# The second expert's output product as seven block products of 512 columns

## The chip, the cores and the metric

The kernel runs on one core of a Trainium2 chip. The metric is device time of one execution in microseconds. TensorE is PE in the rows, its weight loads PEld; VectorE is DVE, ScalarE is ACT, GpSimd is POOL, and SyncE (SP) issues all transfers between the chip's memory and the core's on-chip buffers.

## The reference

Attention over 4 x 576 = 2304 tokens gives 512 features per token. Two experts follow, each of the form below, the first one behind a normalisation. The change touches the second.

```python
def _moe2_ref(x, w_gate, w_val, w_out) -> np.ndarray:
    g = x @ w_gate
    silu = g * (1.0 / (1.0 + np.exp(-g)))
    val = x @ w_val
    return (silu * val @ w_out).astype(np.float32)
```

x is 2304 x 512, the hidden layer has 1536 features, and the result is 2304 x 512.

## The kernel before

Everything is kept transposed: features on the 128 partitions, tokens along the columns. The tokens form five groups (TGROUPS): four of 512 and one of 256. The 1536 hidden features are twelve chunks f of 128 (KF). Products are made in three parts: each float32 operand is split into a rounded high part H (a copy on ACT) and the remainder L (a subtraction on DVE or POOL, L1120), and a product is H.H + H.L + L.H, three matmuls that accumulate in one PSUM bank.

The first layer of the second expert runs over f (`pair_unit` and `plain_unit`). For each f the four wide groups form two pairs, and gate and value of a pair are computed together as a 2 x 2 block product with seven products instead of eight, each of six wide matmuls (L1274). Copies of banks go to buffers on ACT (`keep`, L1280), additions of banks run on DVE (`add`, L1284), one sum of two buffers at L1310. `gated` then makes silu(g) times v as Tanh on ACT (L1289) and two DVE operations (L1291, L1294); the factor one half that this leaves out is applied at the very end (L1141, L1143). The hidden block, 128 x 512, is stored to memory (`h2_d`, L1296). The 256-token group takes 24 narrow matmuls (L1325) and the operations of `hidden`. Weights of f + 2 are fetched, converted from 8-byte floats (L1070 on ACT, L1074 on DVE), summed (L1191) and split (L1198, L1201) by `load_w2`.

The output stage multiplies the hidden layer by w_out (`out_layer`, `out_mm`). For each group it reads twelve hidden blocks back (L1160), splits each (L1117, L1120), and issues twelve matmuls per block: four row blocks of the result by three parts (L1132). Four banks accumulate over the twelve blocks, and are copied out and stored (`out_store`). w_out is loaded and split (`load_o`, L1051, L1053) while the first layer ends and the output stage begins.

The order on each engine is fixed when the program is built: every operation is recorded with its engine, an estimated duration, its operands and a priority, and `Plan.run` lists them greedily, lowest priority number first among those that are ready by its estimates. Each engine then works through its own list in order, and an operation that must wait holds up what stands behind it on that engine.

## Time and profile before

| | |
|---|---|
| runs | 1100.15, 1098.49, 1096.84 us (median 1098.49) |
| the profiled execution | 1097.84 us, of which the span of its records is 1096.1 |
| PE busy | 1078.8 us of the span, 6580 matmuls |
| DVE, ACT, POOL busy | 675.9, 583.5, 208.1 us |
| transfers | 131.42 MB, mean 120 GB/s, none above 512 KB |
| second expert, first layer | 664.1 to 947.4 us of the span |
| second expert, output stage | 940.7 to 1092.6 us, its first rows between the last of the first layer |

The span is what the records cover; the run's own time is 1.7 us longer. Busy time is the union of an engine's records. Matmuls are pipelined, so a single one's record is longer than the distance from one to the next.

### The profile page before, as it was taken

How to read it: one execution, taken by the hardware profiler on the slowest of the kernel's cores; microseconds unless marked ns; L12 is line 12 of the kernel's file. 1: busy time of each engine (PE TensorE's matmuls, PEld its weight loads, DVE VectorE, ACT ScalarE, POOL GpSimd, SP SyncE). 2: the span in 40 equal slices, each digit the busy share in tenths (PEclk: the TensorE clock that was granted, in tenths of full speed). 3: DMA queues.
4: the chain of work that ended last, by engine and by line, in shares of the span. 5: the costliest groups of instructions: out<-in, count | busy, mean ns of one | idle time of the engine just before them, and what ended most of it. 6: DMA issues, size and time to landing. Idle time of an engine off the chain costs nothing.

```text
span 1096.1 us, 19019 instructions
## 1 busy us (share of the span) xinstructions
PE 1078.8 (98%) x6580; PEld 973.5 (89%) x6580; DVE 675.9 (62%) x1755; ACT 583.5 (53%) x1266; POOL 208.1 (19%) x300
## 2 busy tenths in 40 slices
PE   7899999999999999999999999999999999999998
PEld 5599999999999999999978889888888888888888
DVE  7798788796787766652344437676677566632222
ACT  5877777766775764531244336544554455543222
POOL 4344444423333220210000000121122111000000
PEclk9999999999999999999999999999999999999999
DMA  5974444333332213641233333232232223654342
GB/s 159 301 257 136 112 122 126 117 114 94 98 108 75 80 41 121 182 137 47 70 121 96 99 97 93 91 113 85 101 139 101 88 92 129 210 180 132 99 135 96
DMA packets 81616, 131.42 MB, mean 120 GB/s; under 512 B 12848, under 2 KB 42544, under 8 KB 81520
## 3 DMA queue, kind: packets, MB, share of 16 engines
q1 hardware_dynamic: 81520, 130.20, 37.9%
q8 instruction: 52, 0.85, 0.3%
q14 instruction: 44, 0.36, 0.1%
HBM read 97.05 MB, written 33.10 MB: 119 GB/s over the span
## 4 chain that ended last, share of the span: by engine, by line
PE 84%; DMA 3%; DVE 2%; ACT 1%; issue 1%; POOLq 0%; POOL 0%; ACTq 0%; DVEq 0%; SPq 0%
PE mo L921 23%; PE mo L1132 12%; PE mo L1274 10%; PE sps L1274 8%; PE tp L1132 6%; PE sps L1132 6%; PE tp L708 4%; PE tp L692 4%; PE sps L628 4%; PE mo L1325 3%; DMA cvs<-in_w_o 2%; PE tp L1274 1%; PE mo L828 1%; ACT cvy L1070 1%; DVE cvs L1074 0%
## 5 line engine op out<-in xcount | busy, mean ns | idle before, releaser
L921 PE MATMUL mo<-xH,H 128*128 128x320 f32 (+1 forms) x768 | 228.0, 297 | 0.8 <-DVE x L905 0.8
L921 PE MATMUL mo<-xL,H 128*128 128x320 f32 (+1 forms) x768 | 227.8, 297 | 0.0
L921 PE MATMUL mo<-xH,L 128*128 128x320 f32 (+1 forms) x768 | 227.7, 297 | 0.0
L921 PEld LDWEIGHTS mo<-xH,H 128*128 128x128 f32 x768 | 144.1, 188 | 1.9 <-DVE x L905 1.0
L921 PEld LDWEIGHTS mo<-xL,H 128*128 128x128 f32 x768 | 144.3, 188 | 0.7 <-issue 0.2
L921 PEld LDWEIGHTS mo<-xH,L 128*128 128x128 f32 x768 | 144.3, 188 | 0.4
L665 ACT ACTIVATE sc<-sc,col 128x512 f32<-128x512 f32 (+4 forms) x160 | 96.0, 601 | 64.3 <-DVE col L654 63.7
L1120 DVE TENSOR_TENSOR hL<-hh,hH 128x512 fp32r<-128x512 f32 (+1 forms) x90 | 58.2, 651 | 114.8 <-ACT hH L1117 114.6
L1117 ACT ACTIVATE hH<-hh 128x512 fp32r<-128x512 f32 (+1 forms) x90 | 52.5, 587 | 114.9 <-PE mo L1132 55.9
L928 ACT ACTIVATE t<-mo 128x256 f32<-128x256 f32 (+1 forms) x108 | 43.1, 399 | 58.5 <-PE mo L921 57.9
L930 DVE SCALAR_TENSOR_TENSOR t<-t,mo 128x256 f32<-128x256 f32 (+1 forms) x108 | 48.1, 445 | 40.4 <-ACT t L928 39.4
L692 PE MATMUL tp<-ident,sc 128*128 128x128 f32 x432 | 65.5, 276 | 0.0
L700 DVE TENSOR_TENSOR pTB<-tp,pTB 128x512 fp32r<-128x512 f32 (+1 forms) x96 | 54.4, 575 | 14.5 <-ACT pTB L697 12.4
L933 DVE TENSOR_TENSOR hh<-t,mo 128x256 f32<-128x256 f32 (+1 forms) x108 | 48.0, 445 | 18.9 <-PE mo L921 18.0
L1280 ACT ACTIVATE u<-sps 128x512 f32<-128x512 f32 x48 | 28.7, 598 | 54.1 <-PE sps L1274 54.0
L1132 PE MATMUL mo<-hL,oH 128*128 128x512 f32 (+1 forms) x144 | 54.4, 378 | 0.0
L628 PE MATMUL sps<-kHH,qst 128*128 128x288 f32 (+4 forms) x160 | 54.2, 346 | 0.0
L1132 PE MATMUL mo<-hH,oH 128*128 128x512 f32 (+1 forms) x144 | 54.0, 377 | 0.0
L1132 PE MATMUL mo<-hH,oL 128*128 128x512 f32 (+1 forms) x144 | 53.8, 377 | 0.0
L1289 ACT ACTIVATE u<-u 128x512 f32<-128x512 f32 x48 | 29.7, 633 | 43.7 <-DVE u L1284 43.7
L654 DVE CUSTOM_DVE_ANT_0 sc<-sps,cb 128x384 f32<-128x384 f32 (+3 forms) x112 | 48.9, 443 | 6.4 <-PE sps L628 5.3
L697 ACT ACTIVATE pTB<-tp 128x512 fp32r<-128x512 f32 (+1 forms) x96 | 47.0, 502 | 10.9 <-PE tp L692 5.9
(221 smaller groups left out, 2795.3 us busy)
## 6 DMA issues: line engine op xcount, KB each, us to landing
hh<-h_d SPq DMA_DIRECT2D x72, 256.0 KB, 2.6
cvs<-in_w_gv SPq DMA_DIRECT2D x28, 511.8 KB, 4.6
h_d<-u SPq DMA_DIRECT2D x48, 256.0 KB, 2.0
cvs<-in_w_o SPq DMA_DIRECT2D x24, 511.8 KB, 4.0
h_d<-hh SPq DMA_DIRECT2D x84, 128.0 KB, 1.9
raw<-in_w_gv SPq DMA_DIRECT2D x20, 511.8 KB, 5.7
lq<-in_qk SPq DMA_DIRECT2D x32, 288.0 KB, 3.6
cb<-cum_d SPq DMA_DIRECT2D x32, 288.0 KB, 3.5
```

Of the source, the lines that this page charges most:

```text
L628: op(PE, c_mm(n), lambda en, pt=pt, o=o, c=c, n=n, z=z, kk=kk: en.matmul(pt()[:, :n], qst[j]()[:, o:o + 128], kk()[:, c:c + n], start=z == ...
L654: op(DVE, c_tt(w), lambda en: en.tensor_tensor_reduce(out=sc()[:m, c:c + w], in0=pt()[:m, c - at:c - at + w], in1=bias()[:m, c + off:c + o ...
L665: op(ACT, c_act(o + m, 2) + 35, lambda en: en.activation(sc()[:m, :o + m], sc()[:m, :o + m], ACTF.Exp, scale=-1.0, bias=col()[:m, 0, t:t + 1],
L692: op(PE, C_TR, lambda en, pt=pt, a=a, m=m, kb=kb, t=t: en.transpose(pt()[:, a:a + P], self.sc[t]()[:, kb * P:kb * P + P], ident()), r=[sel ...
L700: op(DVE, c_tt(n), lambda en, pt=pt, a=a, d0=d0, n=n, kn=kn: en.tensor_tensor(out=L()[:kn, d0:d0 + n], in0=pt()[:kn, a:a + n], in1=f32(H() ...
L921: op(PE, c_mm(n), lambda en, a=a, x=x, c=c, k=k, i=i: en.matmul(ps()[:, :n], a()[:, c], x()[:, k, :n], start=(k == 0 and i == 0), stop=(k ...
L930: op(DVE, c_tt(n), lambda en: en.scalar_tensor_tensor(out=t()[:, :n], in0=t()[:, :n], scalar=1.0, in1=gp()[:, :n], op0=ALU.add, op1=ALU.mu ...
L933: op(DVE, c_tt(n), lambda en: en.tensor_tensor(out=hh()[:, :n], in0=t()[:, :n], in1=vp_()[:, :n], op=ALU.mult), r=[vp_, t], w=[hh], pri=pri)
L1117: op(ACT, c_act(n) + 35, lambda en: en.activation(H(), src(), ACTF.Copy), r=[src], w=[H], pri=pri)
L1120: lambda en: en.tensor_tensor(out=L(), in0=src(), in1=f32(H()), op=ALU.subtract),
L1132: op(PE, c_mm(n), lambda en, d=d, c=c, w=w, x=x, i=i: en.matmul(acc_[d]()[:, :n], Wo[w]()[:, c], HL[x](), start=(f == 0 and i == 0), stop= ...
L1274: op(PE, c_mm(n), lambda en, w=w, xx=xx, cut=cut, kk=kk, i=i: en.matmul(ps()[:, :n], W[w]()[:, cut], xx(), start=first and kk == 0 and i == 0,
```

## The change

The output product is made for each pair of groups as a 2 x 2 block product too: w_out in four blocks (768 hidden features by 256 outputs), the hidden layer of the pair in four blocks (768 features by 512 tokens). Seven products of six chunks replace eight, with sums S1 to S4 of the w_out blocks and differences T1 to T4 of the hidden blocks. For f from 0 to 5 `pair_unit` stores B12, B11 and their difference T1; for f from 6 to 11 it reads B12 and T1 of f - 6 back and stores B22, B21, T3, T2 and T4. All go to memory as rows of 128 x 512 (`row_d`). The blocks and sums of w_out are made during f = 0 to 5 (`store_o`), stored to `wo_d`, and read back and split later (`fetch_o`) into places that the first layer leaves free. `strassen_out` reads the rows in the order of the products (`fetch_row`, a rotation of four buffers each for the row and its two parts), each row feeding six matmuls, two output row blocks by three parts. The 256-token group is multiplied plainly, last, as before. `gated` and `plain_unit` use Silu on ACT and one DVE product; the factor one half falls away. A buffer that the program reserves for software-made transfer descriptors is cut to 1024 bytes, which makes room.

```diff
-    def pair_unit(f, W, X, groups, pri):
+    def pair_unit(f, W, X, p, pri):
...
-        def gated(g, t, ps, v, gi):
-            op(ACT, c_act(n), lambda en: en.activation(t(), g(), ACTF.Tanh, scale=0.5),
-               r=[g], w=[t], pri=-1.0e4)
-            op(DVE, c_tt(n), lambda en: en.scalar_tensor_tensor(
-                out=t(), in0=t(), scalar=1.0, in1=g(), op0=ALU.add, op1=ALU.mult),
-               r=[g, t], w=[t], pri=-1.0e4, port=True)
-            op(DVE, c_tt(n), lambda en: en.tensor_tensor(out=t(), in0=t(), in1=v(), op=ALU.mult),
-               r=[t, ps], w=[t], pri=-1.0e4, port=ps is u3)
-            op(SP, 4 * P * n, lambda en: en.dma_start(out=h2_d[gi][f], in_=t()), r=[t],
-               w=[(f"h2_d{gi}", f)], pri=-1.0e4)
+        def gated(g, ps, v):
+            op(ACT, c_act(n), lambda en: en.activation(g(), g(), ACTF.Silu),
+               r=[g], w=[g], pri=-1.0e4)
+            op(DVE, c_tt(n), lambda en: en.tensor_tensor(out=g(), in0=g(), in1=v(), op=ALU.mult),
+               r=[g, ps], w=[g], pri=-1.0e4, port=ps is u3)
+
+        def store(name, src):
+            op(SP, 4 * P * n, lambda en: en.dma_start(out=row_d[p, name][k6], in_=src()), r=[src],
+               w=[(f"row{p}{name}", k6)], pri=-1.0e4)
+
+        def fetch(name, dst):
+            op(SP, 4 * P * n, lambda en: en.dma_start(out=dst(), in_=row_d[p, name][k6]),
+               r=[(f"row{p}{name}", k6)], w=[dst], pri=pri)
+
+        def less(out, a, b):
+            op([(POOL, c_ptt(n)), (DVE, c_tt(n) + 60)], 0, lambda en: en.tensor_tensor(
+                out=out(), in0=a(), in1=b(), op=ALU.subtract), r=[a, b], w=[out], pri=-1.0e4,
+               port=True)
+        if f >= K6:
+            fetch("T1", t1)
+            fetch("B12", t2)
...
-        gated(u2, t2, u3, u3, groups[1])
+        gated(u2, u3, u3)
         product(b, "A22", "T4", False)
-        gated(p1, t1, b, lambda: b()[:, :n], groups[0])
+        gated(p1, b, lambda: b()[:, :n])
+        if f < K6:
+            store("B12", u2)
+            store("B11", p1)
+            less(p5, u2, p1)
+            store("T1", p5)
+        else:
+            store("B22", u2)
+            store("B21", p1)
+            less(t2, u2, t2)
+            store("T3", t2)
+            less(t1, u2, t1)
+            store("T2", t1)
+            less(p5, p1, t1)
+            store("T4", p5)
...
+        hh = m2buf(f"tmp{f % 2}", [P, 512], F32, "hh")
+        op(ACT, c_act(n), lambda en: en.activation(hh()[:, :n], gp()[:, :n], ACTF.Silu),
+           r=[gp], w=[hh], pri=-1.0e4)
+        op(DVE, c_tt(n), lambda en: en.tensor_tensor(
+            out=hh()[:, :n], in0=hh()[:, :n], in1=vq()[:, :n], op=ALU.mult),
+           r=[hh, vq], w=[hh], pri=-1.0e4)
+        op(SP, 4 * P * n, lambda en: en.dma_start(out=rest_d[f], in_=hh()[:, :n]),
+           r=[hh], w=[("rest_d", f)], pri=-1.0e4)
...
+    K6 = KF // 2
+    ROWS = ("B11", "B12", "B21", "B22", "T1", "T2", "T3", "T4")
+    row_d = {(p, name): dram.tile([K6, P, 512], F32, name=f"row{p}{name}")
+             for p in range(NPAIR) for name in ROWS}
+    rest_d = dram.tile([KF, P, 256], F32, name="rest_d")
+    O_BLOCKS = ("A11", "A21", "A12", "A22", "S1", "S2", "S3", "S4")
+    wo_d = dram.tile([2, 4, P, K6, 256], F32, name="wo_d")
+
+    def store_o(i, pri):
+
+        vals, osum = (buf("ex", f"ex{z}", [P, 1024], F32, ("vals", "osum")[z]) for z in range(2))
+        for z in range(2):
+            load_raw(w2_o[(i + K6 * z) * P:(i + K6 * z + 1) * P, :], raws[z], pri,
+                     lambda z=z: vals()[:, 512 * z:512 * z + 512], (vals, z))
+        a11, a21, a12, a22 = (Part(vals, k // 2, lambda t, k=k: t[:, 256 * k:256 * k + 256])
+                              for k in range(4))
+        s1, s2, s3, s4 = (Part(osum, k, lambda t, k=k: t[:, 256 * k:256 * k + 256])
+                          for k in range(4))
+        for out, a, b, sign in ((s1, a21, a22, ALU.add), (s2, s1, a11, ALU.subtract),
+                                (s3, a11, a21, ALU.subtract), (s4, a12, s2, ALU.subtract)):
+            op([(POOL, c_ptt(256)), (DVE, c_tt(256) + 60)], 0,
+               lambda en, out=out, a=a, b=b, sign=sign: en.tensor_tensor(
+                   out=out(), in0=a(), in1=b(), op=sign), r=[a, b], w=[out], pri=pri, port=True)
+        for z, t in ((0, vals), (1, osum)):
+            op(SP, 4 * P * 1024, lambda en, z=z, t=t: en.dma_start(
+                out=wo_d[z].rearrange("q p k c -> p q k c")[:, :, i],
+                in_=t().rearrange("p (q c) -> p q c", c=256)), r=[t], w=[("wo_d", (i, z))],
...
-        pair_unit(f, W2[f], X2[0], (0, 1), P3 + 40 * f)
+        pair_unit(f, W2[f], X2[0], 0, P3 + 40 * f)
         plain_unit(f, W2[f], rest, 2 * NPAIR, 256, P3 + 40 * f + 10)
-        pair_unit(f, W2[f], X2[1], (2, 3), P3 + 40 * f + 20)
-
-    W2o = []
-    w2o_wide = {}
+        if f < K6:
+            store_o(f, P3 + 40 * f + 19)
+        pair_unit(f, W2[f], X2[1], 1, P3 + 40 * f + 20)
...
+    plan.live["ex"] = []
+    seats = [seat("ex", f"ex{i}", [P, 1024], 1)[0] for i in range(3)]
+    for tag in w2_tags[0]:
+        seats += seat("m2", tag, [P, 2048], 2)
+    free_w = [f"{z}{f}" for f in range(KF) for z in "HL"]
+    for tag in free_w[:14]:
+        seats += seat("w", tag, [P, 1024], 1)
+    last_seats = [seat("w", tag, [P, 1024], 1)[0] for tag in free_w[14:17]]
...
+    def fetch_o(name, seats, pri, stages=stages):
+
+        q = O_BLOCKS.index(name)
+        for j, (H, L) in enumerate(seats):
+            st = stages[nstage[0] % len(stages)]
+            nstage[0] += 1
+            op(SP, 4 * P * 512, lambda en, st=st, j=j: en.dma_start(
+                out=st().rearrange("p (k c) -> p k c", c=256),
+                in_=wo_d[q // 4, q % 4][:, 2 * j:2 * j + 2]),
+               r=[("wo_d", (i, q // 4)) for i in (2 * j, 2 * j + 1)], w=[st], pri=pri)
+            split(st, 512, H, L, pri)
+        return seats
...
+    PRODUCTS = (("A11", "B11"), ("S1", "T1"), ("S2", "T2"), ("S4", "B22"), ("S3", "T3"),
+                ("A12", "B21"), ("A22", "T4"))
...
+    deep = {"h": [("o", "hh0"), ("o", "hh1"), ("m2", "tmp0"), ("m2", "tmp1")],
+            "H": [("o", "hH0"), ("o", "hH1"), ("o", "oH4"), ("o", "oH5")],
+            "L": [("o", "hL0"), ("o", "hL1"), ("o", "oL4"), ("o", "oL5")]}
...
+    def fetch_row(src, key, n, pri):
+
+        hh, H, L = (dring(z, F32 if z == "h" else F32R) for z in "hHL")
+        def view(b):
+            return Part(b, None, lambda t: t[:, :n])
+        hh, H, L = view(hh), view(H), view(L)
+        op(SP, 4 * P * n, lambda en: en.dma_start(out=hh(), in_=src), r=[key], w=[hh], pri=pri)
+        split(hh, n, H, L, -1.0e4, any_engine=False)
+        return H, L
...
+        def product(ps, first, claims=()):
+            a, x = PRODUCTS[step[0]]
+            at = pri + step[0]
+            step[0] += 1
+            for kk in range(K6):
+                H, L = fetch_row(row_d[p, x][kk], (f"row{p}{x}", kk), n, at)
+                for m in range(2):
+                    for i, (z, xx) in enumerate(((0, H), (0, L), (1, H))):
+                        part, w = weight(a, kk, m, z)
+                        op(PE, c_mm(n), lambda en, m=m, w=w, xx=xx, kk=kk, i=i: en.matmul(
+                            ps[m]()[:, :n], w(), xx(), start=first and kk == 0 and i == 0,
+                            stop=kk == K6 - 1 and i == 2, skip_group_check=not first),
+                           r=[part, xx], w=[ps[m]] if kk or m or i else [*ps, *claims], pri=at)
...
+        product(b, True, c if p == 0 else [])
+        keep(p1, b)
+        product(c, True)
+        keep(p5, c)
+        product(b, False)
+        keep(u2, b)
+        product(c, False)
+        add(u2, c)
+        store(u2, 0, 2 * p + 1)
+        product(b, False)
+        keep(u3, b)
+        for m in range(2):
+            op([(POOL, c_ptt(n)), (DVE, c_tt(n))], 0, lambda en, m=m: en.tensor_tensor(
+                out=u3[m](), in0=u3[m](), in1=p5[m](), op=ALU.add), r=[u3[m], p5[m]], w=[u3[m]],
+               pri=-1.0e4, port=True)
+        store(u3, 1, 2 * p + 1)
+        product(d, True)
+        add(p1, d)
+        store(p1, 0, 2 * p)
...
-    for gi, (t0, n) in enumerate(TGROUPS):
-        a = out_layer(gi, h2_d, f"h2_d{gi}", W2o, P4 + 100 * gi, gi % 2 == 0, True)
...
```

Where the orders differ. PE in the output stage; `oH`, `hH` are high parts of a row (their `L` the remainders), `mo` are banks. Before, one row feeds twelve matmuls:

```order
L1132 MATMUL mo3_11499<-hH0_11528,oH_10835 128x512
L1132 MATMUL mo3_11499<-hL0_11533,oH_10835 128x512
L1132 MATMUL mo3_11499<-hH0_11528,oL_10842 128x512
L1132 MATMUL mo0_11506<-hH0_11528,oH_10835 128x512
L1132 MATMUL mo0_11506<-hL0_11533,oH_10835 128x512
L1132 MATMUL mo0_11506<-hH0_11528,oL_10842 128x512
L1132 MATMUL mo2_11515<-hH0_11528,oH_10835 128x512
L1132 MATMUL mo2_11515<-hL0_11533,oH_10835 128x512
L1132 MATMUL mo2_11515<-hH0_11528,oL_10842 128x512
L1132 MATMUL mo1_11521<-hH0_11528,oH_10835 128x512
L1132 MATMUL mo1_11521<-hL0_11533,oH_10835 128x512
L1132 MATMUL mo1_11521<-hH0_11528,oL_10842 128x512
```

After, six, and the next row follows:

```order
L1531 MATMUL mo2_11272<-oH4_11401,wo_11050 128x512
L1531 MATMUL mo2_11272<-oL4_11406,wo_11050 128x512
L1531 MATMUL mo2_11272<-oH4_11401,wo_11050 128x512
L1531 MATMUL mo1_11281<-oH4_11401,wo_11050 128x512
L1531 MATMUL mo1_11281<-oL4_11406,wo_11050 128x512
L1531 MATMUL mo1_11281<-oH4_11401,wo_11050 128x512
L1531 MATMUL mo2_11272<-oH5_11409,wo_11050 128x512
L1531 MATMUL mo2_11272<-oL5_11416,wo_11050 128x512
L1531 MATMUL mo2_11272<-oH5_11409,wo_11050 128x512
L1531 MATMUL mo1_11281<-oH5_11409,wo_11050 128x512
L1531 MATMUL mo1_11281<-oL5_11416,wo_11050 128x512
L1531 MATMUL mo1_11281<-oH5_11409,wo_11050 128x512
```

Each row is used half as long, for two banks instead of four, and the rotation of rows is four buffers deep (`hH0`, `hH1`, `oH4`, `oH5`) where it was two. PE's whole list has 6250 rows in place of 6322.

DVE at the end of one late f (the second pair's unit), before: two additions of banks, two multiply-adds behind Tanh, the sum, the two gate products:

```order
L1284 TENSOR_TENSOR u_10780<-sps1_10754,u_10780 128x512
L1284 TENSOR_TENSOR u_10757<-tp0_10765,u_10757 128x512
L1291 SCALAR_TENSOR_TENSOR u_10795<-u_10795,u_10780 128x512
L1291 SCALAR_TENSOR_TENSOR u_10799<-u_10799,u_10757 128x512
L1310 TENSOR_TENSOR u_10808<-u_10808,u_10767 128x512
L1294 TENSOR_TENSOR u_10795<-u_10795,u_10808 128x512
L1294 TENSOR_TENSOR u_10799<-u_10799,sps0_10686 128x512
```

After: additions, sum, one gate product, two differences, the gate product of the other half, one difference (the fourth stands on POOL in this f):

```order
L1291 TENSOR_TENSOR u_10720<-sps1_10682,u_10720 128x512
L1291 TENSOR_TENSOR u_10685<-tp0_10695,u_10685 128x512
L1328 TENSOR_TENSOR u_10744<-u_10744,u_10698 128x512
L1298 TENSOR_TENSOR u_10720<-u_10720,u_10744 128x512
L1310 TENSOR_TENSOR u_10627<-u_10720,u_10627 128x512
L1310 TENSOR_TENSOR u_10620<-u_10720,u_10620 128x512
L1298 TENSOR_TENSOR u_10685<-u_10685,sps0_10612 128x512
```

The multiply-adds are gone, and differences stand between and behind the gate products.

SP at the seam of the two stages, before: the last hidden blocks go out between reads for the first group and the loads of w_out:

```order
L1296 DMA h2_d1536_86<-u_10991 128x512
L1160 DMA oH11_11038<-h2_d0_83 128x512
L1296 DMA h2_d1024_85<-u_10996 128x512
L1067 DMA cvs0_6356<-in_w2_o 128x2047
L1160 DMA oL11_11071<-h2_d0_83 128x512
L1067 DMA cvs1_6371<-in_w2_o 128x2047
L1160 DMA hh0_11090<-h2_d0_83 128x512
L1067 DMA cvs0_6356<-in_w2_o 128x2047
L1160 DMA hh1_11123<-h2_d0_83 128x512
```

After: the last f's stores for the second pair stand between reads of T1, and the last of them, T4, ahead of T1's chunks 4 and 5:

```order
L1302 DMA row1B22_97<-u_11138 128x512
L1512 DMA tmp1_11222<-row0T1_90 128x512
L1512 DMA hh1_11232<-row0T1_90 128x512
L1302 DMA row1T3_100<-u_11058 128x512
L1302 DMA row1B21_96<-u_11101 128x512
L1302 DMA row1T2_99<-u_11046 128x512
L1302 DMA row1T4_101<-u_11113 128x512
L1512 DMA tmp0_11270<-row0T1_90 128x512
L1512 DMA tmp1_11285<-row0T1_90 128x512
L1512 DMA hh0_11291<-row0T2_91 128x512
```

The loads of w_out are no longer here; its parts are read from `wo_d` ahead of these rows.

## Rows read from the trace of the kernel before

**Rows 1.** Head of the page; busy us, share of the span, instructions.

```profile
span 1096.1 us, 19019 instructions
...
PE 1078.8 (98%) x6580; PEld 973.5 (89%) x6580; DVE 675.9 (62%) x1755; ACT 583.5 (53%) x1266; POOL 208.1 (19%) x300
```

**Rows 2.** Windows around the change: busy us and count by engine.

```profile
core 0: us, PE busy (x) PEld busy (x) DVE busy (x) ACT busy (x) POOL busy (x), PEclk, DMA share, GB/s
700.00:935.00 235.00, 235.00 (x1161) 199.61 (x1160) 158.97 (x238) 120.04 (x207) 45.45 (x40) 1.00 0.31 109
935.00:955.00 20.00, 20.00 (x90) 16.55 (x89) 13.11 (x22) 11.82 (x19) 0.00 (x0) 1.00 0.66 211
955.00:1040.00 85.00, 84.87 (x373) 69.34 (x371) 26.66 (x39) 29.13 (x48) 0.00 (x0) 1.00 0.44 138
```

**Rows 3.** Waits of PEld, 660 to the end: total us, times, longest.

```profile
PEld mo L1132 <- DVE hL L1120: 0.9, 2, 0.5
```

**Rows 4.** Chain that ended last, in order of time: start us, us, what.

```profile
733.23 2.51 PE mo L1325 x21
...
1010.01 32.64 PE mo L1132 x144
...
1075.29 16.21 PE mo L1132 x135
1091.52 1.50 DVE oo L1143 x4
```

**Rows 5.** Timeline from 1053 (start us, us): one hidden row split.

```profile
1053.57 0.63 ACT L1117 ACTIVATE hH<-hh 128x512 fp32r<-128x512 f32 x1 [2.09 <-PE tp L1132]
...
1054.23 0.69 DVE L1120 TENSOR_TENSOR hL<-hh,hH 128x512 fp32r<-128x512 f32 x1 [2.03 <-ACT hH L1117]
```

**Rows 6.** Line L1160 (reads of hidden rows), 940 to the end.

```profile
DMA to landing us min/median/max: 1.9/2.6/4.7
```

**Rows 7.** Groups of DVE, 700 to 935: busy us, mean ns, idle before.

```profile
L1291 DVE SCALAR_TENSOR_TENSOR u<-u 128x512 f32<-128x512 f32 x44 | 28.7, 688 | 2.8 <-ACT u L1289 0.7
L1201 DVE TENSOR_TENSOR w2L<-sf,w2H 128x512 fp32r<-128x512 f32 x11 | 17.2, 1575 | 0.0
...
L1074 DVE SCALAR_TENSOR_TENSOR cvs<-cvs,cvy 128x512 uint32<-128x512 uint32 x21 | 14.5, 692 | 0.3 <-ACT cvy L1070 0.2
L1310 DVE TENSOR_TENSOR u<-u 128x512 f32<-128x512 f32 x21 | 14.4, 688 | 3.4 <-ACT u L1280 3.3
...
L930 DVE SCALAR_TENSOR_TENSOR t<-t,mo 128x256 f32<-128x256 f32 x11 | 4.6, 414 | 0.0
...
L1191 DVE TENSOR_TENSOR sf<-cvs 128x256 f32<-128x256 f32 x8 | 3.4, 425 | 0.3
```

**Rows 8.** The same for ACT.

```profile
L1289 ACT ACTIVATE u<-u 128x512 f32<-128x512 f32 x44 | 27.2, 632 | 42.1 <-DVE u L1284 42.1
...
L1280 ACT ACTIVATE u<-sps 128x512 f32<-128x512 f32 x41 | 24.6, 599 | 48.0 <-PE sps L1274 47.9
L1070 ACT ACTIVATE cvy<-cvs 128x512 f16<-128x512 bf16 x22 | 17.4, 791 | 4.6 <-DVE cvs L1074 3.9 <-DMA cvs<-in_w_gv 0.7
```

**Rows 9.** Timeline of DVE, 924 to 930.

```profile
925.24 0.69 DVE L1294 TENSOR_TENSOR u<-u,sps 128x512 f32<-128x512 f32 x1 [1.81 <-PE sps L1274]
926.26 1.35 DVE L1053 TENSOR_TENSOR oL<-cvs,oH 128x512 fp32r<-128x512 f32 x1 [0.34 <-ACT oH L1051]
```

**Rows 10.** Timeline of POOL in the same stretch.

```profile
925.75 1.31 POOL L1053 TENSOR_TENSOR oL<-cvs,oH 128x512 fp32r<-128x512 f32 x1 [18.94 <-ACT oH L1051]
```

**Rows 11.** Windows, columns as in Rows 2, of three other stretches.

```profile
38.00:58.00 20.00, 15.86 (x90) 11.30 (x88) 17.38 (x54) 17.46 (x43) 8.92 (x9) 0.91 1.05 332
48.00:50.00 2.00, 2.00 (x7) 1.08 (x6) 1.52 (x6) 1.39 (x5) 1.92 (x2) 0.50 1.09 254
952.00:956.00 4.00, 4.00 (x19) 3.34 (x18) 1.23 (x2) 1.38 (x2) 0.00 (x0) 1.00 0.86 318
```

**Rows 12.** Timeline of ACT at the start: the one load of function tables.

```profile
0.73 1.28 ACT L665 ACT_TABLE_LOAD   x1 [0.73 <-PEq L1433]
```

More of the change, by code (lines that the diff above doesn't have):

```diff
@@ L1263, in pair_unit @@
         n = 512
+        k6 = f % K6
         step = [0]
@@ new lines, in tile_kernel @@
+    n = 256
+    acc_ = [mo_bank() for _ in range(4)]
+    for f in range(KF):
+        H, L = fetch_row(rest_d[f], ("rest_d", f), n, P4 + 200 + f)
+        for dd in range(KD):
+            name = "A11 A21 A12 A22".split()[dd // 2 + 2 * (f // K6)]
+            for i, (z, xx) in enumerate(((0, H), (0, L), (1, H))):
+                part, w = weight(name, f % K6, dd % 2, z)
+                op(PE, c_mm(n), lambda en, dd=dd, w=w, xx=xx, f=f, i=i: en.matmul(
+                    acc_[dd]()[:, :n], w(), xx(), start=f == 0 and i == 0,
+                    stop=f == KF - 1 and i == 2), r=[part, xx],
+                   w=[acc_[dd]] if f or dd or i else acc_, pri=P4 + 200 + f)
@@ L1432 @@
     }
[L1433 removed]
+    nc = bacc.Bacc("TRN2", target_bir_lowering=False, num_devices=1, dynamic_dma_scratch_size=1024)
     args = [
```

113 lines of the change are left out of this document (84 added, 29 removed).

## The prediction

> **What bounds the kernel now.** I read the page's head first: of a span of 1096.1 us TensorE (PE) is busy 98% [rows 1]. An average over stages says little, so next come windows of the two stages that the change touches [rows 2]. In the second expert's first layer (700 to 935 us) PE is busy all 235.00 us at a granted clock of 1.00, VectorE (DVE) 158.97 (68%), ScalarE (ACT) 120.04 (51%), and the transfers move 109 GB/s. In the output stage (955 to 1040) PE has 84.87 of 85 us. The reader is to see that PE has no hole in either. The waits say the same from the other side: from 660 us on, the only sizeable wait of PE's side is 0.9 us for a DVE split at the seam of the two stages [rows 3]. So the end is set by how many matmuls there are, as long as everything that feeds PE stays ahead of it.
>
> The chain of waits gives the price of one [rows 4]. One group of 512 tokens in the output stage is 144 matmuls in 32.64 us: **226.7 ns** each. The group of 256 columns has 135 in 16.21 us: 120.1 ns. (The 389 ns that a single matmul shows elsewhere overlap with the next one.) So one f of the first layer, 84 matmuls of 512 columns and 24 of 256, is 84 x 0.2267 + 24 x 0.1201 = 21.92 us, and the chain's 2.51 us for 21 narrow ones fits.
>
> **Removed.** Each pair of token groups took 288 wide matmuls in the output stage. Seven products of 6 chunks, 2 row blocks and 3 float parts take 252. Two pairs: 72 fewer. 72 x 0.2267 = **-16.3 us**, all of it on the path, since PE never waits there. The order of PE after the change has just 72 rows less, so that part is certain. The 256-token group keeps its 144. The end behind the last matmul (four copies in 1.50 us [rows 4], then the stores) has the same shape.
>
> **Added in the first layer, off the path.** The gate loses a DVE multiply-add: four of 0.688 us and one of 0.414 per f [rows 7], 3.17 us. I take Silu at Tanh's 0.632 us (between a copy's 0.599 and Tanh plus the multiply-add, 1.32) [rows 7, 8]. Late f (6 to 11) get eight differences, of which the order puts seven on DVE: 7 x 0.688 = 4.8 us. DVE goes from 158.97/235 x 21.92 = 14.8 us per f to 16.5, 75%. One difference goes to POOL, where such an operation takes 1.31 us, and the DVE subtraction beside it took 1.35 instead of 0.69 [rows 9, 10]: 78% at worst. Early f (0 to 5) get two differences, two conversions (0.692) and four short sums (0.425) [rows 7], some 16.1 us of DVE, and two conversions on ACT (0.791 [rows 8]), 12.8 us of ACT, 58%. The cover is PE's 21.92 us per f. If it were gone, the next unit's accumulator bank would come free late. Price: from nothing to one DVE operation (0.69) for each of the 12 late pair units, 8 us; nearest is today's 68% without one wait, so I take 0. The new table load (1.28 us [rows 12]) falls into ACT's idle half: 0.
>
> **Added on the transfers.** A late f now stores ten blocks of 256 KB and reads four, beside 128 KB and two weight loads of 512 KB: 4.85 MB in 21.92 us, 221 GB/s, against 109 now [rows 2]. At full share the transfers moved 332 GB/s over 20 us [rows 11], so this fits, but no longer easily. SP issues in order, and a store that waits for DVE holds back the reads queued behind it.
>
> **The seam** is the tightest place. The order of SP has 25 transfers (6.42 MB) from the store of row B22 to that of T4 of the last f, which spans 61 wide and 24 narrow matmuls and a tail of four DVE operations, about 2.7 us: 16.7 + 2.7 = 19.4 us, or 331 GB/s, right at the 332. Behind that last T4 store wait the reads of T1's chunks 4 and 5. PE reaches chunk 4 after 43 more wide matmuls, 9.75 us. The chain to it: product, split and difference on DVE 2.3 with hand-overs, store issue 0.3, landing 2.6 (at most 4.7 [rows 6]), split 0.63 + 0.69 [rows 5]: 6.5 to 8.6 us. It holds with 1 to 3 us to spare. If the transfers fell to the lowest full-share rate, 254 GB/s [rows 11], 6.42 MB would take 25.3 us, 5.9 late, some 4 of it on PE. The change also moves the weight conversions away from this place, where PE waits 0.9 us today [rows 3]. So the seam costs from -0.9 to +4; I take **+1**, nearer to the rows in which transfers keep up.
>
> **The output stage itself.** A 256 KB row feeds 12 matmuls (2.72 us) today and 6 (1.36 us) after: 193 GB/s, and 230 with the output stores, below the 318 at share 0.86 in 952 to 956 [rows 11]. Four buffers rotate, so a row has 4 x 1.36 = 5.44 us for landing 2.6, split 0.63 + 0.69 [rows 5, 6] and some 0.3 of handing over, 4.2 in all: 1.05 us per row. Per pair DVE does 42 splits, four additions and two sums of 0.69, 33 of 57 us; ACT 42 x 0.63 and ten copies of 0.60, 32.5 us. I take 0, with 0 to 10 as bounds (landing at 4.3 throughout would make 1.48 us per row, 84 x 0.12 = 10).
>
> **Sum** against the profiled execution (1097.84 us, span 1096.1): -16.3 + 1 = 1082.5. That execution lies 0.65 us below the median of the runs shown, 1098.49, so I predict **1083**.
>
> **The rivals.**
> (a) Part of the gain is given back, 4 to 12 us, at the seam or by rows that land near 4.3 us: 1086 to 1094. For it: 331 GB/s against 332, and a DVE at 75%. Against it: the spare time worked out above. Chance 0.20.
> (b) Slower: the output stage becomes bound by the supply of rows. Place: the reads of rows by fetch_row. With four buffers a row takes (landing + 1.62)/4. The gain is gone at 1.36 + 16.3/84 = 1.555 us per row, that is from a landing of 4.6 us, and 4.7 is the longest seen [rows 6]. If twice the traffic doubles the landing to 5.2, a row takes 1.71 us, 84 x 0.345 = 29 us, and the time is 1110. A PE that idles may lose clock as well: in 48 to 50 us, after PE had been idle, the granted clock was 0.50, the lower of its two levels, 1.2 GHz of 2.4 [rows 11]. Against it: 318 GB/s without a full share. Chance 0.05.
> (c) Rows are served one after another: 2.6 us each, 84 x (2.6 - 1.36) = 104 us, about 1186. The trace speaks against it, since 2.6 us for 256 KB is 101 GB/s, and 318 needs three at a time [rows 6, 11]. Chance 0.01.
> The Trainium skill (DMA: Bandwidth & Descriptors, Measured) says "Batch DMAs to ≥1 MiB for ≥75% of peak", which speaks against a stage that doubles the rate of its 256 KB reads; this trace does not bear it out here, with 332 GB/s where no transfer is above 512 KB [rows 11].
> (d) The gain is returned nearly whole by several small waits: within 0.3%. Chance 0.04. That the products are not fewer is excluded by the order.
> (e) Better than 1081, if the seam's 0.9 goes too and the measured runs are low: 0.02.
>
> **How the numbers follow.** The forecast has 0.68. 0.3% is 3.3 us, about what a measurement of this kernel can tell from no change. Faster: 0.68 + 0.02 + nearly all of (a), 0.19, makes 0.89. Same: (d) and the end of (a), 0.05. Slower: (b) and (c), 0.06. The range begins at 1080.5 (nothing given back, less 0.9 and some spread of the runs) and reaches to 1093, which takes in most of (a) and leaves out about 0.15.
>
> **What would show it.** PE busy through windows of the first layer at 21.9 us per f, with DVE near 75% in its second half; a product of 36 matmuls in 8.16 us, at the same 226.7 ns; reads of rows landing at 3 us or so; the last matmul 15 us earlier. Wrong at the seam: PE waiting there for a split behind a late read of T1. Wrong in the stage: regular waits of PE for the DVE split of a row, rows above 1.36 us apart, landings above 3.8 us. Wrong in the first layer: PE waiting for DVE or ACT at the start of a pair unit.

## The result, and the profile after

The changed kernel takes 1086.73 us (median of four runs, 1084.75 to 1088.33) against 1098.93 for the kernel before in the same comparison: ratio 0.989, interval 0.9867 to 0.9913. It is faster by 12.2 us, 1.1%, where 1083, 15.5 less, was forecast. The profiled execution took 1088.33 us.

Head of the page of the changed kernel, the counterpart of [rows 1]:

```profile
span 1086.5 us, 19382 instructions
...
PE 1064.3 (98%) x6508; PEld 960.5 (88%) x6508; DVE 725.7 (67%) x1827; ACT 611.1 (56%) x1319; POOL 213.2 (20%) x300
```

PE has 72 matmuls fewer and 14.5 us less busy time, yet the span fell by 9.6. Windows (columns as in [rows 2]) show where PE has holes that it did not have before:

```profile
788.00:810.00 22.00, 22.00 (x110) 18.68 (x109) 16.54 (x25) 12.09 (x22) 4.30 (x4) 1.00 0.67 220
810.00:832.00 22.00, 21.21 (x103) 17.22 (x101) 17.01 (x27) 13.37 (x25) 2.84 (x2) 1.00 0.74 244
832.00:854.00 22.00, 21.53 (x106) 18.31 (x107) 18.50 (x27) 11.49 (x21) 5.60 (x4) 1.00 0.70 244
854.00:876.00 22.00, 22.00 (x110) 18.68 (x109) 17.07 (x25) 10.89 (x20) 4.31 (x3) 1.00 0.63 218
...
950.00:960.00 10.00, 8.34 (x35) 5.92 (x33) 8.37 (x12) 6.60 (x14) 1.67 (x1) 1.00 0.93 316
960.00:970.00 10.00, 9.65 (x41) 7.58 (x42) 7.64 (x13) 6.92 (x14) 0.00 (x0) 1.00 0.82 242
985.00:1060.00 75.00, 75.00 (x333) 62.10 (x332) 43.79 (x66) 40.95 (x67) 0.00 (x0) 1.00 0.77 234
```

The holes are around f 6 (810 to 854) and at the seam (950 to 970). The output stage behind it is full, at 234 GB/s, and its chain of waits is made of products of 36 matmuls in 8.16 us, 226.7 ns each:

```profile
960.86 31.49 PE mo L1531 x137
992.34 8.16 PE sps L1531 x36
...
1065.78 16.93 PE mo L1596 x141
```

PE's idle time understates a hole, since a matmul after a stop also takes longer (0.50 us instead of 0.39 at 826.93). The same group of narrow matmuls in the two chains tells it better. Of the kernel before, at f 4 and at f 10 (start, us):

```profile
777.15 2.51 PE mo L1325 x21
...
908.91 2.51 PE mo L1325 x21
```

Of the changed kernel:

```profile
779.75 2.27 PE mo L1357 x19
...
913.38 2.51 PE mo L1357 x21
```

The group ends at 779.66 before and 782.02 after, 2.36 us later; six f on, at 911.42 and 915.89, 4.47 later. So **2.1 us** are lost in between. (At f 4 the chain cuts the 24 narrow matmuls at two places, after 21 and after 19. Counted by pair matmuls, 84 to an f, the 505th starts 2.38 us later than before and the 589th 4.46, which gives the same 2.1.) The first 2.3 us are not counted as the change's: the first expert's output stage already began 2.6 us later (438.06 against 435.45), and in the profiled executions of all twelve kernels told of here that start lies anywhere between 435.45 and 438.06.

To be free of that, every run below is read by three times of its trace: the first and the last start of a matmul of the pair units (L1274 before, L1281 after), and the start of the last matmul of all.

| kernel | first, last pair matmul | layer | last matmul | from last pair matmul |
|---|---|---|---|---|
| before | 664.2, 947.2 | 283.0 | 1092.3 | 145.1 |
| after | 666.5, 952.7 | 286.2 | 1082.8 | 130.1 |

The rows with the last and the first start of a pair matmul (durations in ns, then first and last start in us), before and after:

```profile
L1274 PE MATMUL sps<-xHT,w2L x96: 389/389/393, 694.4 to 947.2; 128*128 128x512 f32 x96
...
L1274 PE MATMUL mo<-xHB,w2H x72: 389/389/396, 664.2 to 927.8; 128*128 128x512 f32 x72
```

```profile
L1281 PE MATMUL sps<-xHT,w2L x96: 389/389/398, 696.6 to 952.7; 128*128 128x512 f32 x96
...
L1281 PE MATMUL mo<-xHB,w2H x72: 389/389/396, 666.5 to 932.2; 128*128 128x512 f32 x72
```

From first to last it is 428.1 before and 416.3 after: 11.8 less, about the 12.2 of the medians. 16.3 were removed, and **4.5 came back: 3.2 in the first layer** (2.1 around f 6, the rest at its very end) **and 1.3 at the start of the output stage** (145.1 - 16.3 = 128.8 would be nothing lost). The line between the layer and what follows it is good to about half a microsecond: 17 matmuls of the output stage stand ahead of the last pair matmul in both kernels, and 15 to 18 in the runs below, at 0.23 us each.

### The profile page after: what moved, and what is told of

Read it like the earlier page. It is cut to its first block, busy times and chain, and to the rows that moved or that the text cites. A ratio compares the mean times of both kernels' runs of the same rounds, so it can differ in the third digit from the quotient of the medians.

```text
span 1086.5 us, 19382 instructions
## 1 busy us (share of the span) xinstructions
PE 1064.3 (98%) x6508; PEld 960.5 (88%) x6508; DVE 725.7 (67%) x1827; ACT 611.1 (56%) x1319; POOL 213.2 (20%) x300
## 4 chain that ended last, share of the span: by engine, by line
PE 80%; DMA 5%; DVE 3%; ACT 2%; issue 1%; SPq 0%; ACTq 0%; DVEq 0%
PE mo L922 23%; PE mo L1281 9%; PE sps L1281 7%; PE mo L1138 6%; PE mo L1531 5%; PE tp L709 4%; PE tp L693 4%; PE sps L629 4%; PE tp L1138 3%; PE sps L1138 3%; PE tp L1531 3%; PE mo L1357 2%; DMA cvs<-in_w_gv 2%; PE mo L1596 2%; PE sps L1531 2%; DMA cvs<-in_w_o 1%
## 5 line engine op out<-in xcount | busy, mean ns | idle before, releaser
L922 PE MATMUL mo<-xH,H 128*128 128x320 f32 (+1 forms) x768 | 228.4, 298 | 0.6 <-DVE x L906 0.6
L1126 DVE TENSOR_TENSOR hL<-hh,hH 128x512 fp32r<-128x512 f32 (+1 forms) x108 | 71.1, 662 | 93.6 <-ACT hH L1123 93.3
L1123 ACT ACTIVATE hH<-hh 128x512 fp32r<-128x512 f32 (+1 forms) x108 | 63.9, 595 | 102.5 <-PE mo L1138 38.5
L929 ACT ACTIVATE t<-mo 128x256 f32<-128x256 f32 (+1 forms) x96 | 38.5, 401 | 56.6 <-PE mo L922 56.4
L931 DVE SCALAR_TENSOR_TENSOR t<-t,mo 128x256 f32<-128x256 f32 (+1 forms) x96 | 43.1, 449 | 39.1 <-ACT t L929 38.2
L701 DVE TENSOR_TENSOR pTB<-tp,pTB 128x512 fp32r<-128x512 f32 (+1 forms) x96 | 54.4, 575 | 14.4 <-ACT pTB L698 12.2
L1074 ACT ACTIVATE cvy<-cvs 128x512 f16<-128x512 bf16 x48 | 38.0, 791 | 45.9 <-DMA cvs<-in_w_gv 30.3
L934 DVE TENSOR_TENSOR hh<-t,mo 128x256 f32<-128x256 f32 (+1 forms) x96 | 43.1, 449 | 20.0 <-PE mo L922 16.2
L693 PEld LDWEIGHTS tp<-ident,sc 128*128 128x128 f32 x432 | 50.3, 141 | 0.3
L643 POOL TENSOR_SCALAR_AFFINE_SELECT sc<-cb 128x128 f32<-128x128 f32 (+1 forms) x128 | 37.7, 322 | 62.7 <-PE tp L693 41.9
L1126 DVE TENSOR_TENSOR oL<-tmp,oH 128x512 fp32r<-128x512 f32 (+1 forms) x48 | 31.6, 658 | 27.5 <-ACT oH L1123 27.4
```

Source lines behind the costliest of these rows:

```text
L693: op(PE, C_TR, lambda en, pt=pt, a=a, m=m, kb=kb, t=t: en.transpose(pt()[:, a:a + P], self.sc[t]()[:, kb * P:kb * P + P], ident()), r=[sel ...
L701: op(DVE, c_tt(n), lambda en, pt=pt, a=a, d0=d0, n=n, kn=kn: en.tensor_tensor(out=L()[:kn, d0:d0 + n], in0=pt()[:kn, a:a + n], in1=f32(H() ...
L922: op(PE, c_mm(n), lambda en, a=a, x=x, c=c, k=k, i=i: en.matmul(ps()[:, :n], a()[:, c], x()[:, k, :n], start=(k == 0 and i == 0), stop=(k ...
L1123: op(ACT, c_act(n) + 35, lambda en: en.activation(H(), src(), ACTF.Copy), r=[src], w=[H], pri=pri)
L1126: lambda en: en.tensor_tensor(out=L(), in0=src(), in1=f32(H()), op=ALU.subtract),
```

## What PE waited for

Waits of PE from 655 us to the end, changed kernel (total us, times, longest); before, the same view lists none in this stretch:

```profile
PE sps L1281 <- ACT u L1287: 1.5, 2, 0.8
PE mo L1531 <- DVE oL L1126: 0.8, 2, 0.5
PE mo L1531 <- ACT oH L1123: 0.6, 1, 0.6
PE mo L1281 <- ACT u L1287: 0.4, 1, 0.4
```

L1287 is `keep`, the copy on ACT that frees an accumulator bank; L1123 and L1126 are the two operations of a split. The chain of waits of the changed kernel shows what stood ahead of `keep` near f 6:

```profile
824.15 5.42 DMA cvs<-in_w_gv
...
829.65 0.80 ACT cvy L1074
...
831.85 0.58 ACT u L1287
...
832.47 3.01 PE sps L1281 x12
```

and the timeline of ACT at both places:

```profile
829.65 0.79 ACT L1074 ACTIVATE cvy<-cvs 128x512 f16<-128x512 bf16 x1 [2.50 <-DMA cvs<-in_w_gv]
831.20 0.78 ACT L1074 ACTIVATE cvy<-cvs 128x512 f16<-128x512 bf16 x1 [0.76 <-DVE cvs L1078]
831.85 1.05 ACT L1287 ACTIVATE u<-sps 128x512 f32<-128x512 f32 x2
...
949.21 0.63 ACT L1123 ACTIVATE wo<-wst 128x512 fp32r<-128x512 f32 x1 [1.76 <-DMA wst<-wo_d]
949.74 0.62 ACT L1296 ACTIVATE u<-u 128x512 f32<-128x512 f32 x1
950.27 0.61 ACT L1123 ACTIVATE wo<-wst 128x512 fp32r<-128x512 f32 x1
950.79 0.57 ACT L1287 ACTIVATE u<-sps 128x512 f32<-128x512 f32 x1
```

ACT is idle for 2.50 us, and works in the order that the planner wrote: the conversion of raw weights is at its head, the read for it has not landed, and the copy behind it, which needs nothing of that read, holds a bank that PE wants. At 949.21 it is the same with the split of an output-weight block (1.76 us).

The shorter wait at f 6, 0.42 us at 826.93, came about through DVE. The copy that freed that bank (826.30) stood behind a gate on ACT, and the gate waited for an addition on DVE:

```profile
824.72 0.63 ACT L1296 ACTIVATE u<-u 128x512 f32<-128x512 f32 x1 [2.49 <-DVE u L1291]
```

DVE had stood idle for 0.49 us until a late conversion, and from 818.13 on worked with no listed pause through sums, splits and differences before it came to that addition (824.01). So a late read reaches PE by two ways: at once, where the conversion stands ahead of `keep` on ACT, and a few us later, where DVE has to catch up.

At the seam comes the sign that the prediction named, PE at a split behind a late read of T1 (issued 954.04, landed after 5.3 us):

```profile
959.45 0.63 ACT L1123 ACTIVATE oH<-tmp 128x512 fp32r<-128x512 f32 x1 [3.40 <-DMA tmp<-row0T]
```

It is not the chain that the prediction had worked out. The reads behind the T4 store are those of T1's chunks 4 and 5; this one is issued 4 us ahead of the T2 and T4 stores, and PE waited with it at the 43rd matmul of the stage, in T1's chunk 1:

```profile
954.04 0.32 SPq L1512 DMA_DIRECT2D tmp<-row0T  x1
...
958.27 0.88 SPq L1302 DMA_DIRECT2D row1T<-u  x2
```

The chunks behind the T4 store (issued 959.25 and 960.83) came without a wait.

The planner (`Plan`, which writes each engine's order by estimated durations) reckons 2.3 us plus the size over 350 GB/s to a landing: 3.8 us for 512 KB, 3.05 for 256 KB. The reads above took 5.42, 4.49 (issued 944.69) and 5.3.

**Theory**: in the first layer ACT's fixed order has too little slack for the reads' real arrival. **Rivals**: DVE, at 78% in the late f, makes banks late (the prediction's own bound); the crowd of reads that begins at f 6; at the seam, the rate of the transfers, or the tail of differences on DVE.

## The experiments

Each edit is against the changed kernel, unless said. The table at the end has all times.

**1. A11's weights and the first rows read later.**

```diff
-               r=[("wo_d", (i, q // 4)) for i in (2 * j, 2 * j + 1)], w=[st], pri=pri)
+               r=[("wo_d", (i, q // 4)) for i in (2 * j, 2 * j + 1)] +
+               ([("rest_d", K6 + 1)] if name == "A11" else []), w=[st], pri=pri)
```

> Only the order changes: the six reads of block A11 of the output weights, and with them the first rows of the output stage that take over their staging buffers, come two steps of f later (behind the sixth hidden chunk that the 256-token group writes in the second half), so that they no longer fall on the change from the first to the second half of the layer. In the changed kernel PE falls 2.1 us behind between f 5 and f 7. Theory (the read of w2_gv is issued late, because SP stands behind reads of rows that wait for their buffers; ACT stands at the conversion of those weights, and the copy that frees PE's bank stands behind it): the 2.1 us go or shrink below 0.7, the total falls by 1.4 to 2.1 us to about 1085, with PE at 22.00 of 22 us in 810 to 832. Rival 1 (the differences, which begin at f 6, make DVE late): PE still loses about 2 us at f 6, no gain. Rival 2 (it moves with the reads): the same 2 us at f 8 or 9, no gain.

1086.58 us: no gain; the layer takes 286.1. (A11 is three reads, not the six of the expectation.) Nor is it rival 2: nothing is lost at f 8 or 9. Of the loss at f 6 only 0.5 us of idle PE is left (21.50 of 22 us in 810 to 832), but 700 to 810, full before, now has a hole of 0.75. Timeline of ACT there, first of the changed kernel, then of this one:

```profile
772.12 0.79 ACT L1074 ACTIVATE cvy<-cvs 128x512 f16<-128x512 bf16 x1 [0.97 <-DMA cvs<-in_w_gv]
```

```profile
771.91 0.79 ACT L1074 ACTIVATE cvy<-cvs 128x512 f16<-128x512 bf16 x1 [2.09 <-DMA cvs<-in_w_gv]
```

The same conversion at the same place in the order waited 2.09 us instead of 0.97, and then it reached PE, by way of DVE (idle 1.96 us until 772.73, a gate on ACT that waited 2.94 us for it, PE's wait of 0.50 us at 781.30). So ACT stands at raw weights in many f; which of these waits reaches PE changes from run to run and order to order. Taking away the crowd at f 6 does not help.

**2. The last four weight blocks read behind the seam.** The same line, with `[("row1T4", K6 - 1)]` added for S4, S3, A12 and A22.

> Only the order changes: the twelve reads (3.1 MB) of the output-weight blocks S4, S3, A12 and A22 come behind the last store of a difference, that is out of the seam and into the second and third product of the output stage. Theory (the seam is short of transfer time: PE's bank there is late because ACT stands at the split of a block whose read lands late, and then T1's rows land late): the loss at the seam, 2.3 us against the kernel before, falls below 1, and the total by 1.3 to 2.3 us to about 1085; transfers in 940 to 955 fall from 300 to about 200 GB/s. Rival (the chain that sets the seam is product, gate, differences on DVE, store of T4, read back): PE waits as long as now, total the same within 0.5 us. A third way: the reads moved into the output stage, 230 GB/s plus 3.1 MB in some 16 us = 420 GB/s, cannot fit there, PE waits in the second or third product, and the total is the same or up to 4 us more.

1089.24 us, 2.5 more: the third way. Windows of this run:

```profile
942.00:950.00 8.00, 8.00 (x37) 6.63 (x36) 3.93 (x7) 4.06 (x7) 0.00 (x0) 1.00 0.39 129
950.00:960.00 10.00, 10.00 (x45) 8.26 (x44) 6.32 (x10) 4.83 (x8) 0.00 (x0) 1.00 0.94 297
960.00:970.00 10.00, 8.67 (x36) 6.23 (x34) 7.80 (x12) 7.76 (x15) 0.00 (x0) 1.00 0.95 315
970.00:980.00 10.00, 7.75 (x30) 5.51 (x31) 8.00 (x13) 8.82 (x16) 0.00 (x0) 1.00 0.95 336
```

With 3.1 MB gone the seam is clean (PE 18.00 of 18 us in 942 to 960), so its loss did come with those reads. But the output stage cannot take them: PE loses 3.6 us in 960 to 980, at 315 and 336 GB/s.

**3. The planner reckons later landings; the same work.** In `Plan`, with `slow=True` at the reads of raw weights in `load_raw` and of blocks in `fetch_o`:

```diff
+    SLOW = 1500.0
...
-            done = 2300.0 + took - ns
+            done = 2300.0 + took - ns + (self.SLOW if slow else 0.0)
```

> The same work; only the planner that writes the order reckons 1.5 us more for the landing of each read of raw weights and of output-weight blocks (it reckons 2.3 us plus size over 350 GB/s, 3.8 us for 512 KB; the profile shows 5.2, and 4.1 against 3.05 for the blocks). Theory (PE's losses are ACT standing at a conversion whose read is later than planned, with the copy that frees a bank behind it): with conversions placed later in ACT's queue both losses shrink, f 6 from 2.1 to under 1, the seam from 2.3 to under 1.5, total 1 to 3 us less, 1084 to 1086; waits of ACT for cvs and wst during the second expert's first layer fall from about 10 us or more to half. Rival (the loss is DVE's load or the transfers' rate, not the order): total the same within 0.7 us.

1081.25 us: 5.5 less than the changed kernel, more than any theory gave. The layer takes 283.1 instead of 286.2. The edit does more than move conversions within ACT's list: in 700 to 800 us the lists of DVE, POOL and SP come in another order too, and in 700 to 935 DVE is busy 168.72 us instead of 172.21 and POOL 55.87 instead of 47.22. It also reaches back before the layer: the first expert's output stage, from its first matmul to the first pair matmul, takes 226.9 us (435.7 to 662.6) instead of 228.4 (438.1 to 666.5).

**4. Raw weights alone, and 3.0 us.** `slow=True` at `load_raw` only; and `SLOW = 3000.0` at both.

> The changed kernel with 1.5 us more reckoned for the reads of raw weights alone, not for the output-weight blocks that are read back. If the conversions of raw weights in ACT's queue were what held up the banks in the first layer, the 2 us at f 6 are won back here, and the first layer takes 283.2 us from its first to its last matmul (286.2 in the changed kernel); the seam stays at a loss of 1.3 to 2.3: total about 1083 to 1085. Rival (the order of the block reads is what counts): no gain, 1086 to 1087.

> The changed kernel with 3.0 us more reckoned for reads of raw weights and of blocks, in place of 1.5. Landings are 1.2 to 1.4 us later than the planner reckons, in the median, up to about 3 at worst. Theory (the slack only has to cover the real landing): no further gain in the first layer, which already stands at 283.2 us; the seam, with reads of up to 6.3 us to landing, may win up to 1; total 1080 to 1082. Rival (a conversion placed too late holds the buffers longer and delays the next reads): the total rises again, 1083 to 1086.

1082.59 and 1080.99 us. With raw weights alone the layer takes 283.9: that is the part that counts. With 3.0 us it takes 283.0, but two matmuls of the output stage fewer stand in it; counted alike it is 283.4, 0.4 more than in the kernel before. The view of PE's waits has one sort left from 655 us on:

```profile
PE mo L1532 <- DVE oL L1127: 0.4, 2, 0.2
```

The waits of ACT for raw weights in 700 to 935 us (total, times, longest) put the causes in order. Kernel before, changed kernel, raw weights alone, both by 1.5 us:

```profile
ACT cvy L1070 <- DMA cvs<-in_w_gv: 0.7, 1, 0.7
```

```profile
ACT cvy L1074 <- DMA cvs<-in_w_gv: 22.9, 14, 4.2
```

```profile
ACT cvy L1075 <- DMA cvs<-in_w_gv: 9.1, 5, 3.4
```

```profile
ACT cvy L1075 <- DMA cvs<-in_w_gv: 8.5, 6, 3.9
```

With 3.0 us there is no such row at all. The traffic is not lower (232 GB/s in 700 to 935, against 227 in the changed kernel), DVE's load hardly (169.59 us of 235, against 172.21), and PE stood idle for 0.13 us there:

```profile
700.00:935.00 235.00, 234.87 (x1159) 199.20 (x1158) 169.59 (x259) 128.70 (x222) 49.79 (x39) 1.00 0.69 232
```

**5. The kernel before with the same 1.5 us** for raw weights.

> The kernel before, with 1.5 us more reckoned by the planner for each read of raw weights; the work is the same. Control for the run of the changed kernel in which this took 5.5 us off. Theory (the change uses up the slack that the order had, so late reads cost only after it): PE had no wait in the first layer here, so nothing is won there; at the seam at most its 0.9 us; total within 1.5 us of 1098.8. Rival (late landings cost both kernels alike, so the 5.5 us are no part of what the change gave back): total 3 to 5 us less.

1096.27 us, ratio 0.9978 (0.9967 to 0.9989), 2.1 less than the kernel before in the same comparison (1098.38): a little beyond what the theory allowed. The layer takes 283.0 as before; 1.0 goes at the seam (144.1 against 145.1; PE's wait there was 0.9 [rows 3]), 1.4 in the first expert's output stage (437.0 to 664.4, 227.4 us, against 228.8). So the program was not free of this before, but the first layer was. Against this kernel the changed one is **13.7 us** faster by the medians with the very same edit (raw weights alone, 1082.59), 15.0 where the blocks are reckoned later too, and 15.3 with 3.0 us. From the first pair matmul to the last matmul these take 413.9, 413.0 and 412.8 us, against 427.1 here: 13.3 to 14.3 less. The kernel before takes 428.1.

**6. Tanh and multiply-add again in the pair units.** The factor 0.5 is left out.

```diff
-            op(ACT, c_act(n), lambda en: en.activation(g(), g(), ACTF.Silu),
-               r=[g], w=[g], pri=-1.0e4)
+            op(ACT, c_act(n), lambda en: en.activation(p5(), g(), ACTF.Tanh, scale=0.5),
+               r=[g], w=[p5], pri=-1.0e4)
+            op(DVE, c_tt(n), lambda en: en.scalar_tensor_tensor(
+                out=g(), in0=p5(), scalar=1.0, in1=g(), op0=ALU.add, op1=ALU.mult),
+               r=[g, p5], w=[g], pri=-1.0e4, port=True)
```

> The gate of the pair units goes back to Tanh and a multiply-add on DVE (the factor 0.5 is left out, so the output of these tokens is twice the reference's): four DVE operations of 0.69 us more per f, 2.75 us, DVE in the second half from 17.2 of 22 us to about 20, 91%. Theory of the prediction (DVE is covered by PE up to its full time; what PE lost was late reads): the first layer loses at most 2 us more, total 1086 to 1089. Rival (at 78% DVE is already what makes banks late, so load on DVE costs at once): the twelve late pair units lose 0.7 us each, 8 us or more, total from 1094; the Silu gate would then be what makes room for the differences.

1095.12 us, 8.4 more: the theory's 1086 to 1089 missed, and the total that the rival gave, but not at its place. The layer costs 2.9 more (289.1), where the theory allowed 2 and the rival wanted 8, and the seam 4.4 (134.5). Windows at the seam:

```profile
950.00:960.00 10.00, 6.46 (x27) 4.39 (x25) 9.56 (x15) 7.00 (x13) 1.66 (x2) 1.00 0.93 319
960.00:970.00 10.00, 9.50 (x33) 7.09 (x34) 7.46 (x13) 3.79 (x7) 0.00 (x0) 0.83 0.80 243
```

DVE has 9.56 of 10 us, and the longest wait of PE there, 2.0 us, is for DVE.

**7. Tanh with the late plan** (edits 3 and 6).

> Tanh and multiply-add in the pair units (output twice the reference's for their tokens), with the planner reckoning 1.5 us more for reads of raw weights and of blocks. Tanh alone cost 8.4 us against the changed kernel, 2.9 of it in the first layer and 4.4 at the seam. Theory (a busier DVE has less slack for late reads, so the two act together): most of the 8.4 us goes too, total 1082 to 1086. Rival (DVE at 91% costs by itself, at the seam above all, where its tail ends last): 6 to 8 us above the run with the late plan and Silu, total 1087 to 1090.

1084.06 us: of the 8.4 only 2.8 are left over the Silu kernel with the same plan (1.0 in the layer, 1.4 at the seam). In 700 to 935 DVE is busy 194.88 us, 83%, more than in run 6 (189.78), and PE has 234.56 of 235. So DVE's load is covered by PE nearly whole even so, as the prediction held, and two thirds of what it cost came through the order.

**8. Three differences left out.** For f from 6 on T3, T2 and T4 are not subtracted; their stores write u2, u2 and p1.

```diff
-            less(t2, u2, t2)
-            store("T3", t2)
-            less(t1, u2, t1)
-            store("T2", t1)
-            less(p5, p1, t1)
-            store("T4", p5)
+            store("T3", u2)
+            store("T2", u2)
+            store("T4", p1)
```

> The three differences T3, T2 and T4 of the second half are left out (their stores write the undiminished gated rows, so the output of four token groups is not the reference's); reads, stores and their sizes stay. DVE loses six operations of 0.69 us per f from f 6 on, 4.1 of its 17.2 us, and the tail behind the last pair unit loses three. Theory (PE's 2 us in the first layer is ACT standing at a conversion whose read lands later than planned): that loss stays at 1 to 2 us, and the seam wins at most the tail, 1 to 2 us; total 1084.5 to 1086.5, and ACT's waits for raw weights in 700 to 935 us stay near 20 us. Rival (the differences' load on DVE makes the banks late in the first layer and the rows late at the seam): both losses go, total 1082 or below.

1087.57 us: nothing won, and above the 1084.5 to 1086.5 of the theory. The layer loses 4.0 us (287.0) with less work on DVE than any other version had (150.80 us in 700 to 935), and ACT's waits are still there:

```profile
ACT cvy L1074 <- DMA cvs<-in_w_gv: 18.8, 11, 4.7
```

So less load on DVE, with the same reckoning of landings, takes nothing off the layer's loss: that rival is out as the cause, though DVE is one of the two ways by which a late read reaches PE. The seam won 0.8 (129.3), under the 1 to 2 expected: the tail of differences is not what sets it.

**9. Three buffers instead of four for the rows of the output stage.**

```diff
-    deep = {"h": [("o", "hh0"), ("o", "hh1"), ("m2", "tmp0"), ("m2", "tmp1")],
+    deep = {"h": [("o", "hh0"), ("o", "hh1"), ("m2", "tmp0")],
```

and so for H and L.

> The rows of the output stage rotate through three buffers in place of four. By the prediction's formula a row takes (landing + 1.62) / buffers: with 3.0 us to landing, (3.0 + 1.62) / 3 = 1.54 us against the 1.36 that PE needs, 84 x 0.18 = 15 us more, total about 1102, PE waiting at nearly each row, landings near 3.0. If landings fall to 2.5 at the lower rate, 1.37 us, no loss. Rival (the next read is given out well before a buffer's split ends, or landings fall): within 3 us of 1086.7. Above 1108 the hand-overs cost more than 1.62 us, and four buffers were nearer to their limit than the prediction reckoned.

1099.08 us, 12.4 more, where 15 was expected. The profiled execution took 1103.04, 4.0 above the median, and in it what follows the last pair matmul grew by 16.4 us, 0.195 for each of 84 rows, 1.56 us per row against the formula's 1.54. Landings (min, median, max) of the changed kernel and of this one:

```profile
DMA to landing us min/median/max: 1.9/3.0/5.3
```

```profile
DMA to landing us min/median/max: 1.9/2.8/5.6
```

So the sum comes near, but not in the way that the formula has it, with every row held up. PE does not wait at nearly each row: the median distance from row to row behind the seam is 1.38 us, and the mean of 1.55 comes from some twenty late rows. The three longest waits of PE there, 2.40, 1.10 and 1.15 us at 992.86, 1026.50 and 1059.58, are 4.7 of 5.3 us from 975 us on, each behind reads that took 4.3 to 5.6 us to land, and behind the first of them the clock fell too (below). With four buffers, reads of 4.0 to 5.0 us at 1041 to 1046 cost no wait. What the fourth buffer buys, as these two traces show it, is above all cover for late landings; the formula's 1.16 us per row (3.0 us to landing) is an estimate of the mean, 0.2 us below PE's 1.36.

| kernel | us | layer | from last pair matmul |
|---|---|---|---|
| before, 1.5 us later (5) | 1096.27 | 283.0 | 144.1 |
| A11 later (1) | 1086.58 | 286.1 | 130.1 |
| four blocks later (2) | 1089.24 | 284.7 | 133.8 |
| plan 1.5 us later (3) | 1081.25 | 283.1 | 129.9 |
| raw weights only (4) | 1082.59 | 283.9 | 130.0 |
| plan 3.0 us later (4) | 1080.99 | 283.0 | 129.8 |
| Tanh (6) | 1095.12 | 289.1 | 134.5 |
| Tanh, plan later (7) | 1084.06 | 284.1 | 131.3 |
| no differences (8) | 1087.57 | 287.0 | 129.3 |
| three buffers (9) | 1099.08 | 285.2 | 146.5 |

The runs were compared with the kernel before in three sets, in which it took 1098.84, 1098.38 and 1098.21 us. The layer of the last run is, in its order, that of the changed kernel: 285.2 against 286.2 is how far such a loss varies by itself.

**The best version** is the changed kernel with the planner's landings 3.0 us later: 1080.99 us (1080.45 to 1084.10), 0.9849 of the kernel before (0.9831 to 0.9867). The 1.5 us version cannot be told from it.

## Why the prediction was right, and which term was not

- **Removed, -16.3 us**: right. A product is 36 matmuls in 8.16 us, and no row of the output stage came late once the seam was over.
- **The first layer, taken as 0 of bounds 0 to 8**: this is the term that was mis-sized; it measured 3.2. The prediction's sums of work were close: DVE 16.54 of 22 us in an early f and 17.07 in a late one, where 16.1 and 16.5 to 17.1 were worked out, and 218 GB/s in a late f where it was 221. Around f 6 they were not: 244 GB/s, since the first reads of A11 and of output rows fall there, which the sum of 4.85 MB leaves out, and up to 18.50 us of DVE (832 to 854); beside an operation on POOL one of DVE took up to 1.81 us (821.68, L1310), where 1.35 instead of 0.69 had been reckoned. It named the symptom ("the next unit's accumulator bank would come free late") but priced it by DVE's load, and "today's 68% without one wait, so I take 0" does not follow, since load was not the cause: leaving out load won nothing (8), and another order with nearly the same load won back all but about half a microsecond (3, 4). That it is the conversions' place on ACT, and not another part of the new order, is argued from ACT's waits, which went with the loss; no run moved them alone. The step that failed was to check only whether each engine and the transfers had time, and not what stands ahead of `keep` in ACT's queue and how long after the planner's reckoning a read lands.
- **The seam, +1 of -0.9 to +4**: measured +1.3 against the kernel before. That +1 came so near is in part luck. The sign was right, PE at a split behind a late read of T1, but the chain was not: the chunks behind the T4 store came in time, as worked out, and the late read was that of chunk 1, issued ahead of the store, which took 5.3 us where 2.6 to 4.7 had been reckoned for a landing. A second wait there, ACT at the split of a block, was not foreseen, and counts in the 3.2 of the layer's end. That the seam is short of transfer time is shown by run 2, in which it is clean without 3.1 MB of reads. What is left of the seam under the best plan, 1.0 us over 128.8 (0.6, counted alike), was not taken apart.
- **The output stage, 0**: right. The formula for the rows gave the size of run 9 within 3 us, but not its waits: it reckons with one landing time for all rows, and a few late ones cost most. In rival (b), 29 us on top of 1083 make 1112, not 1110.
- Put together, -16.3 + 1 = -15.3 was forecast, and 13.7 to 15.3 less by the medians, 13.3 to 14.3 by the traces, is what the change gives where the planner leaves slack in both kernels (3 and 4 against 5). The changed kernel as it stands loses the layer's 3.2 us besides. That is rival (a) in size, at the seam only in part; its other place, rows landing near 4.3 us, did not come about (3.0).

Not settled: how much of a late conversion is a read that lands slowly and how much one that SP issued late. At 829.65 the landing took 5.42 against 3.8 reckoned, 1.6 of the 2.50 us, and the chain shows that the read was issued at 824.15 when a split of weights on DVE (823.41, L1207) gave its buffer free; over the layer the median landing of raw weights is 4.6 us, against 4.2 before, a small difference for 22.9 us of waits against 0.7. No run separated the two.
